# An expert's last 96 slots as moving columns, fills on another engine, a bound taken by matmul, and a new written order

## The chip, the cores and the metric

The kernel runs on one core of one Trainium2 chip. A core has a matmul engine (TensorE, PE in the rows; its weight loads are listed apart as PEld), a vector engine (VectorE, DVE), an activation engine (ScalarE, ACT), a general engine (GpSimd, POOL) and a queue engine (SyncE, SP) that issues most of the transfers. Each engine works through its own list of instructions in order and waits on semaphores for the others. The metric is the device time of one execution in microseconds (us); the kernel before took 974.89 us as the median of three runs (974.52 to 978.32).

## The reference

Three stages follow one another.

```python
# 1. attention: B=4, H=8, S=576, D=64, pooled by 4 and local in a band
out_d = sm_attn(q_d, k_d, v_d)                 # q, k, v averaged over 4 positions
out_up = np.repeat(out_d, 4, axis=2)
mask = np.abs(pos[:, None] - pos[None, :]) < 4
out_local = softmax(where(mask, q @ k.T / 8, -1e9)) @ v
x = (out_up + out_local) laid out as 2304 tokens x 512
# 2. a dense layer, 512 -> 2048 -> 512
x = maximum(x @ w_in, 0) ** 2 @ w_out
# 3. eight experts, 512 -> 1024 -> 512, the two best of a noisy gate per token
noisy = x @ w_gate + log1p(exp(x @ w_noise)) * noise
for e in range(8):
    out[mask] += top2_w[mask] * (maximum(x[mask] @ w1[e], 0) @ w2[e])
```

The inputs q, k, v and the dense weights are 64 bits wide where they are doubles; the attention inputs are read as 32 bits, the dense weights are turned from 64 to 32 bits on the chip.

## The kernel before

All matmuls of the layers are done with operands that are split into two 16-bit parts, a high and a low one, so that each product takes three matmuls (high by high, high by low, low by high). The scale of each operand comes from a bound on its size. For the two weights of the dense layer and for v this bound is a sum of squares or the largest element of a Gram matrix.

*First stage and dense layer.* One program text, the string `ORDER`, sets in which order the pieces are issued; every engine then has its instructions in that order. A piece is a letter code and a number. `qk`, `vg`, `vw` load inputs; `G` averages q and k; `S` and `D` are the score matmuls of a unit (batch, pair of heads, half of the sequence); `ml`, `md`, `el`, `ed`, `nl`, `nd` are its softmax; `PT` transposes the probabilities, `PW` multiplies them with v, `xb` writes the two halves of x. `vm` takes the bound of v, `vs` its sums, `Xa`, `Xm`, `Xb` make its scale. `il`, `ia`, `ib`, `ic`, `ij` turn one eighth of w_in from 64 to 32 bits (load, two VectorE and two ScalarE steps), `in` adds its Gram matrix, `is` takes the maximum, `wS`, `wT`, `wU` make the scale s_in, `wh` and `wl` write the high and the low half of one eighth of the columns. `ol` to `oo` do the same for w_out. `M` i is the first matmul of the dense layer for one of 72 steps (9 chunks of 256 tokens, 8 groups of 256 hidden columns each), `r` its ReLU and square, `yh` and `yl` the second matmul of chunk 0 in pieces by columns, `Y` and `Z` that of the other chunks. `ga` to `gg` are the gate of one of 18 tiles of 128 tokens: scale, split, transpose (by TensorE and a ScalarE copy for the last tile, L728 and L729), logits (`gd`, L740), a polynomial for log1p(exp) (`gf`), the two best, their slots (`ge`, the prefix sums at L800 and L802) and the scatter of the row into a table in device memory that has 608 slots for each expert.

*Experts.* Expert 0 starts inside `ORDER`: `pe` pieces split its weights, `cm` are its first layer (8 column groups for the first 384 slots, 8 for the last 224) and `cw` its second layer on single tiles of 128 slots, while the last gate tiles still run. Experts 1 to 7 are a plain loop behind it, whose instructions are put in order by the framework's scheduler. For each expert the first layer (L932) runs over 16 pieces, ScalarE and VectorE write the halves of h from PSUM (L934, L935), and between them the weights of the next expert are squared (L861, which waits for their transfer) and split (L877, L878). Then `c_m2` is called for j = 0 to 4, four tiles of 128 slots and one of 96:

```python
for f in range(8):
    do = slice(f * DM, f * DM + DM)
    for a, bb in ((hh, wh), (hh, wl), (hl, wh)):
        nc.tensor.matmul(po, a[:, f, jo], bb[:, do], start=(i == 0), stop=(i == 23))
```

The slots are the stationary operand there and 512 weight columns move, whatever the number of slots. VectorE scales the result with the slot's weight (L950), GpSimd scatters it with an adding transfer (L951). The last tile of expert 7 is done in two halves of 256 columns (`last_m2`, L975 to L979). A final branch for experts with more than 608 slots is not taken.

*Start.* `constants()` makes index ramps, masks and the identity on VectorE and then fills five tiles that must be zero outside what is written later (L159 to L162).

Of the kernel before, what the change touches and what calls it, by code (L numbers as in the profile page):

```python
# [24 lines left out]
E = 8  # L25
# [32 lines left out]
oB2 PW3 in7 oa3 is7 el5 oc2 wS0 ml6 wT0 ol1 oj2 wU0 xb3 oa0 wh1 oB0 oB3 vw5 nl5 wh5 wl1 oc0 oj0 wh0 wl0 os0 wh3
oc3 oj3 oa1 qk4 oB1 os2 wl5 wh2 wl3 wh6 wh7 os3 el6 M5 oc1 oj1 qk5 wl7 ed6 of3 ra5 os1 wh4 nl6 M0 wl6 wl4 vm5
wl2 S7 r0 of1 PW4 nd5 oh2 oo2 ol5 oh3 oh0 vs5 oo3 M1 ra1 ol6 oh1 oo0 G4 D7 M4 ol7 PT5 xb4 nd6 yh0 yl9 M3 r4 md7  # L60
ra3 PW5 yl1 yl0 yh9 oa5 M6 oa6 oo1 yl13 oB5 ml7 ol4 xb5 r6 yl8 yl11 yl3 oa7 S8 yl12 PT6 yl4 ed7 el7 oB6 vg6 M2
oB7 yh6 yh8 ml8 oc5 nl7 yh4 M7 oj5 yh13 oc6 D8 oc7 oj6 yh11 oj7 yh3 oa4 vm6 yh1 oB4 os7 os5 yh14 vw6 md8 yl14
nd7 oc4 os6 qk6 yl6 oj4 S9 of7 PW6 ed8 os4 yh5 oh7 yl5 yh12 qk7 G5 oh6 of5 yh30 vw7 oo7 yh28 vw8 S11 yh27 oh5
oh4 vs6 yh24 yh25 oo5 yh22 PT7 D9 oo4 yh19 oo6 yh20 yh16 xb6 PW7 r2 yh29 yh17 SD0 xb7 yl22 yl29 yl16 yl28 yl24
ml9 vg7 el8 md9 pz0 nl8 yl25 vm7 yh21 yl30 M13 yh2 Xa1 nd8 el9 yl17 G7 ra7 M9 yl18 ed9 D11 yl27 nl9 yh10 Xm1 S10
G6 Xb1 yl2 yh31 nd9 yh15 ra13 pg0 md11 yh18 yh7 vs7 yl10 PT8 D10 PT9 vw9 ip0 ml11 pf0 ra9 md10 ml10 M12 ip1 r12
el10 nl10 yl15 ed10 PW8 yl7 el11 M11 pf1 M10 nd10 ed11 pf2 pf3 yh23 ra11 S12 xb8 D12 yl21 md12 vg8 yl26 nl11 r10
PT10 PW9 ml12 pf4 yl20 M15 vm8 S13 nd11 xb9 el12 vw10 PT11 ml13 D13 ed12 PW10 pf5 md13 vw11 nl12 ra15 M14 xb10
PW11 S15 M8 ed13 el13 S14 nl13 yl23 nd12 r14 pf6 nd13 xb11 r8 D15 PT12 yh26 M16 vw12 yl31 ml14 pf7 zo0 vs8 ra16
el14 md15 PT13 yl19 ga0 gb0 D14 M17 PW12 M19 nl14 ga1 Y8 md14 gc0 Y9 Y10 ml15 Y11 vw13 gb1 ed14 el15 gd0 Y12 vg9  # L70
qk8 nd14 ed15 vw14 Y13 Y14 qk9 vm9 gf0 G8 xb12 G9 ge0 ra17 S16 gc1 gd1 gg0 nl15 M23 vs9 S17 PW13 nd15 Y15 ra19
ra23 qk10 xb13 PT14 vw15 M22 PT15 D16 vg10 ga2 M18 gf1 gb2 ge1 gg1 ra22 PW14 ml16 gc2 qk11 ra18 vm10 ga3 D17
# [27 lines left out]
def moe_kernel(ctx, tc, qk_in, vwin, vgrp, w_in, w_out, w_gate, w_noise, noise, w1, w2, out):  # L100
# [95 lines left out]
    def load_vg(b, hp):  # L196
        if hp == 0:
            vd[b] = ap.tile([72, NP, 4, 64], F32, tag="vd", name=f"vd{b}")
            vmx[b] = ap.tile([P, H], F32, tag="vmx", name=f"vmx{b}")
            nc.vector.memset(vmx[b], 1.0e-30)  # L200
# [840 lines left out]
    def win_pieces():  # L1041
# [343 lines left out]
```

## Time and profile before

| | |
|---|---|
| median of three runs | 974.89 us |
| the profiled execution | 974.24 us, of which the span of its instructions is 972.5 us |
| TensorE busy | 916.3 us (94%) |
| VectorE busy | 580.7 us (60%) |
| ScalarE busy | 498.9 us (51%) |
| GpSimd busy | 132.4 us (14%) |
| transferred | 121.17 MB, mean 125 GB/s |

The span runs from the first to the last instruction; the execution's own time is 1.74 us longer. A share of busy time is an average: the table says that TensorE is nearly always at work, and not where it isn't. The rows further down are stretches, single instructions and pieces of the chain of work that ended last. In them a time in front is the start in us from the span's start, the next is the length of the row, and a bracket gives the idle time of that engine before the row and what ended it. Matmuls are pipelined and the end of each is modelled, so what a matmul costs the next one is read from the distance of starts.

### The profile page before, as it was taken

The numbers are of one execution on the slowest core, as the hardware profiler recorded it, in microseconds if no ns is written. First come the engines' busy times: TensorE is split into PE (matmuls) and PEld (weight loads), VectorE is DVE, ScalarE is ACT, GpSimd is POOL, SyncE is SP. The second block draws the span as 40 slices with busy tenths as digits, with TensorE's granted clock in tenths as the row PEclk, the third lists the DMA queues.
The fourth block names the chain that finished last, engine by engine and source line by source line (L and its number), as shares of the span: only waits on it lengthen the run. The fifth ranks groups of instructions, "written<-read, shape, count | busy, mean of one in ns | idle before, by whom it ended". The sixth has DMA issues, their size and how long they took to land.

```text
span 972.5 us, 20336 instructions
## 1 busy us (share of the span) xinstructions
PE 916.3 (94%) x8278; PEld 619.0 (64%) x8278; DVE 580.7 (60%) x1812; ACT 498.9 (51%) x1076; POOL 132.4 (14%) x151
## 2 busy tenths in 40 slices
PE   4549999999999899999999979999999999999997
PEld 2437988675766567676757546746565565656574
DVE  7989887488678666566477765543435262626221
ACT  5688767455466455455744472753626263624010
POOL 2501100011102010010111121020111111110203
PEclk9768999999999999999999999999999999999999
DMA  9942587923241502013411748771847667590304
GB/s 290 337 147 97 169 262 287 240 90 86 88 101 58 86 30 49 21 61 96 161 56 36 226 122 222 122 206 20 221 56 204 73 187 90 158 119 10 43 1 55
DMA packets 103143, 121.17 MB, mean 125 GB/s; under 512 B 68256, under 2 KB 68448, under 8 KB 100992
## 3 DMA queue, kind: packets, MB, share of 16 engines
q1 hardware_dynamic: 94544, 100.30, 38.0%
q0 software_dynamic: 8496, 19.48, 10.0%
q8 instruction: 67, 1.10, 0.5%
q14 instruction: 36, 0.29, 0.1%
HBM read 70.33 MB, written 35.02 MB: 108 GB/s over the span
## 4 chain that ended last, share of the span: by engine, by line
PE 65%; DVE 4%; ACT 2%; DMA 1%; issue 0%; POOL 0%; POOLq 0%; ACTq 0%; DVEq 0%
PE po L948 20%; PE phc L932 19%; PE y L663 11%; PE ph L617 11%; DMA xs<-row,si 1%; ACT xall L861 1%; PE px L429 1%; PE px L421 1%; PE pol L975 1%; PE S L310 0%; PE S L295 0%; PE pfr L479 0%; PE ptp L375 0%; PE pl L740 0%; ACT r L636 0%
## 5 line engine op out<-in xcount | busy, mean ns | idle before, releaser
L617 PE MATMUL ph<-xall,wih 128*128 128x256 f16 x1152 | 196.1, 276 | 0.6 <-ACT r L636 0.4
L932 PEld LDWEIGHTS <-we 128*128 128x128 f16 x1536 | 148.5, 98 | 50.7
L948 PE MATMUL po<-we,h 128*128 128x512 f16 (+1 forms) x816 | 177.3, 379 | 0.0
L617 PE MATMUL ph<-xall,wil 128*128 128x256 f16 x576 | 158.6, 275 | 2.0 <-DVE wil L1095 2.0
L932 PE MATMUL phc<-xT,we 128*128 128x384 f16 (+1 forms) x1152 | 150.6, 293 | 0.0
L948 PEld LDWEIGHTS <-h 128*128 128x128 f16 (+1 forms) x816 | 83.4, 102 | 91.2
L663 PE MATMUL y<-wo,gh 128*128 128x512 f16 x448 | 133.3, 379 | 0.0
L617 PEld LDWEIGHTS <-wih 128*128 128x128 f16 x1152 | 111.1, 99 | 18.4 <-issue 1.9
L934 ACT ACTIVATE h<-phc 128x384 f16<-128x384 f32 (+1 forms) x112 | 47.3, 423 | 135.3 <-PE phc L932 135.3
L950 DVE TENSOR_SCALAR ob<-po,om 128x512 f32<-128x512 f32 (+1 forms) x34 | 25.5, 749 | 122.8 <-PE po L948 122.8
L832 POOL DMA_INDIRECT xs<-row,si x36 | 38.6, 1072 | 403.1 <-issue 110.3
L951 POOL DMA_INDIRECT out_dram<-ob,tk x34 | 52.3, 1538 | 298.6 <-DVE ob L950 284.2
L935 DVE SCALAR_TENSOR_TENSOR h<-phc,h 128x384 f16<-128x384 f32 (+1 forms) x112 | 52.2, 470 | 64.9 <-ACT h L934 64.9
L663 PE MATMUL y<-wo,gl 128*128 128x512 f16 x224 | 84.9, 379 | 0.3 <-DVE gl L646 0.3
L663 PEld LDWEIGHTS <-gh 128*128 128x128 f16 x448 | 42.1, 98 | 44.6 <-issue 1.0
L646 DVE TENSOR_TENSOR gl<-g,gh 128x512 f16<-128x512 f32 x64 | 44.3, 693 | 39.7 <-ACT gh L645 39.3
L617 PEld LDWEIGHTS <-wil 128*128 128x128 f16 x576 | 56.9, 99 | 9.8 <-DVE wil L1095 2.5
L636 ACT ACTIVATE r<-ph 128x512 f32<-128x512 f32 x72 | 42.2, 586 | 13.2 <-PE ph L617 13.0
L640 ACT ACTIVATE g<-r 128x512 f32<-128x512 f32 x72 | 45.4, 630 | 2.3
L861 ACT ACTIVATE junk<-w1raw 128x1024 bf16<-128x1024 f32 x24 | 25.4, 1056 | 36.4 <-DMA w1raw<-in_moe_w_dram 25.8
L878 DVE SCALAR_TENSOR_TENSOR we<-w1raw,sce,we 128x1024 f16<-128x1024 f32 x32 | 40.6, 1278 | 2.7 <-ACT we L877 2.7
L878 DVE SCALAR_TENSOR_TENSOR we<-w2raw,sce,we 128x1024 f16<-128x1024 f32 x32 | 40.6, 1275 | 0.9 <-ACT we L877 0.9
(354 smaller groups left out, 1382.3 us busy)
## 6 DMA issues: line engine op xcount, KB each, us to landing
w1raw<-in_moe_w_dram SPq DMA_DIRECT2D x8, 2048.0 KB
w2raw<-in_moe_w_dram SPq DMA_DIRECT2D x8, 2048.0 KB
xs<-zrow SPq DMA_DIRECT2D x8, 1290.0 KB
qkT<-in_qk_dram SPq DMA_DIRECT2D x16, 579.0 KB
raw<-in_moe_w_out_dram SPq DMA_DIRECT2D x8, 1024.0 KB
out_dram<-zrow SPq DMA_DIRECT2D x1, 4864.0 KB
raw<-in_moe_w_in_dram SPq DMA_DIRECT2D x4, 1024.0 KB
vw<-in_vwin_dram SPq DMA_DIRECT2D x48, 76.0 KB
```

The costliest lines, as they stand in the source:

```text
L617: nc.tensor.matmul(ph[:, f], a[:, kk, fo], bb[:, kk], start=(n == 0), stop=(n == 11))
L636: nc.scalar.activation(r, ph, AF.Relu, scale=KAPPA)
L640: nc.scalar.activation(g, r, AF.Square)
L646: nc.vector.tensor_tensor(gl, g, gh, op=OP.subtract)
L663: nc.tensor.matmul(py[c, tt], a[:, o], bb[:, ft], start=(ft == 0 and n == 0), stop=(ft == 15 and n == 2))
L832: st = nc.gpsimd.indirect_dma_start(out=xs, out_offset=bass.IndirectOffsetOnAxis(ap=si[:, kk:kk + 1], axis=0), in_=roww, in_offset=None)
L878: nc.vector.scalar_tensor_tensor(wl[:, o], raws[i][:, o], ss[i], wh[:, o], op0=OP.mult, op1=OP.subtract)
L932: nc.tensor.matmul(ph[:, :n], a[:, fo], xT[:, bb], start=(i == 0), stop=(i == 11))
L934: nc.scalar.activation(hh[:, f], ph[:, :n], AF.Relu)
L935: nc.vector.scalar_tensor_tensor(hl[:, f], ph[:, :n], 0.0, hh[:, f], op0=OP.max, op1=OP.subtract)
L948: nc.tensor.matmul(po, a[:, f, jo], bb[:, do], start=(i == 0), stop=(i == 23))
L951: st = nc.gpsimd.indirect_dma_start(out=out, out_offset=bass.IndirectOffsetOnAxis(ap=tk[:m], axis=0), in_=ob[:m], in_offset=None, compute_ ...
```

## The change

Five things are changed.

- The second layer of the tile of 96 slots of experts 1 to 7 is done the other way round. `part_m2` takes 128 weight columns as stationary operand and moves the 96 slots, in four groups of 24 matmuls, into one PSUM bank (`poT`). ScalarE copies the result (`yt`), `part_rows` transposes it back with four matmuls against the identity (`poR`), and VectorE and GpSimd go on as before. The tiles are taken in the order 0, the matmuls of the 96 slots, 1, their transposes, 2, 3; expert 7 ends with tile 3 in two halves.
- The five fills of `constants()` run on GpSimd.
- The bound of v for batch 0 is the largest element of a Gram matrix of the 72 rows, made by 32 matmuls into one PSUM tile, in place of eight squares on ScalarE.
- The Gram matrices of w_in go into one PSUM tile instead of four, so one maximum is taken in place of four and one over them; the bound of a quarter of w_out is a maximum and no longer a sum over the diagonal.
- `ORDER` is written anew, with the gate's `gf` split into `gx`, `gy` and `gz`.

```diff
@@ ORDER, first line and the lines about the last gate tile
-vg0 vg3 ob0 qk0 vg2 S0 vg1 vm0 qk1 qk2 vm1 vm2 G0 S1 ml0 G1 D0 md0 ml1 el0 vg4 ed0 S2 vm3 G2 vm4 el1 D1 il0 Xa0
+qk0 vg0 G0 qk1 S0 S1 ml0 D0 G1 il0 el0 nl0 vg2 qk2 D1 ml1 md0 ed0 vm0 nd0 vg4 md1 ia0 vg1 el1 S2 ed1 ib0 S4 G2
...
-gc17 le1 cm1 gd17 ge16 gx17 cm6 pe17 gg16 gy17 gz17 cm5 pe18 ge17 gg17 cm4 pe19 pe20 cm3 pe21 pe22 pe23 pe24 cw1
+cm2 gx16 cm7 gc17 gy16 cm0 gz16 le1 cm1 gd17 gx17 cm6 ge16 gy17 cm5 gg16 gz17 cm4 cm3 ge17 gg17 pe17 pe18 pe19
@@ constants()
         nc.gpsimd.memset(pms[0], 0.0)
+        for i in range(2):
+            nc.gpsimd.memset(pTs[i][0], 0.0)
+            nc.gpsimd.memset(vws[i][32:64], 0.0)
...
-        nc.vector.memset(pms[1], 0.0)
-        for i in range(2):
-            nc.vector.memset(pTs[i][0], 0.0)
-            nc.vector.memset(vws[i][32:64], 0.0)
+        nc.gpsimd.memset(pms[1], 0.0)
@@ vg_max, x_scale
+        v = vg.rearrange("g a b -> g (a b)").bitcast(BF16).rearrange("g (f n w) -> g f n w", n=P, w=2)[:, :, :, 1]
+        for f in range(8):
+            nc.tensor.matmul(pv0[:, :P], v[:, f], v[:, f], start=(seen_v[0] == 0), stop=(seen_v[0] == 31))
+            seen_v[0] += 1
...
-        nc.vector.tensor_reduce(m1, vmx[b], AX.X, OP.max)
+        nc.vector.tensor_reduce(m1, vmx[b] if b else pv0[:, :P], AX.X, OP.max)
@@ second layer of the 96 slots
+    def part_m2(e, hh, hl):
+        _, (wh, wl) = WE[e][0]
+        jo = slice(NR * P - P, CAP)
+        m = CAP - jo.start
+        po = ps2.tile([P, DM], F32, tag="m2", name="poT")
+        for d in range(4):
+            i = 0
+            for f in range(8):
+                do = slice(f * DM + d * P, f * DM + d * P + P)
+                for a, bb in ((wh, hh), (wh, hl), (wl, hh)):
+                    nc.tensor.matmul(po[:, m * d:m * d + m], a[:, do], bb[:, f, jo], start=(i == 0), stop=(i == 23))
+                    i += 1
+        yt = cp.tile([P, 4, m], F32, tag="yt", name="yt", bufs=1)
+        nc.scalar.activation(yt.rearrange("p d m -> p (d m)"), po[:, :4 * m], AF.Copy)
+        return yt
+
+    def part_rows(e, yt, om, tk, ob):
+        m = CAP - (NR * P - P)
+        pt = psT.tile([P, 512], F32, tag="tp", name="poR")
+        for d in range(4):
+            nc.tensor.transpose(pt[:m, P * d:P * d + P], yt[:, d], idf)
+        nc.vector.tensor_scalar(ob[:m], pt[:m], om[:m], None, op0=OP.mult)
+        scatter(e, tk, ob, m)
@@ Gram matrices of w_in and w_out
-                nc.tensor.matmul(pn[i][:, P * (f % 4):P * (f % 4) + P], v[:, f], v[:, f], start=i in fresh,
-                                 stop=done_[i] == 16)
+                nc.tensor.matmul(pn[:, P * (f % 4):P * (f % 4) + P], v[:, f], v[:, f], start=done_[0] == 1,
+                                 stop=done_[0] == 64)
...
-            for i in (2 * c, 2 * c + 1):
-                nc.vector.tensor_reduce(top[:, i:i + 1], pn[i], AX.X, OP.max)
+            if c:
+                nc.vector.tensor_reduce(top, pn, AX.X, OP.max)
...
-                nc.vector.scalar_tensor_tensor(pq[:, P:2 * P], pq[:, :P], 1.0, idf, op0=OP.mult, op1=OP.mult,
-                                               accum_out=acc[q_][:, c:c + 1])
+                nc.vector.tensor_reduce(acc[q_][:, c:c + 1], pq[:, :P], AX.X, OP.max)
@@ loop over experts 1 to 7
-        for j in range(NR):
+        for j in (0, NR - 1, 1, NR, 2, 3):
+            if j == NR - 1:
+                yt = part_m2(e, hh, hl)
+                continue
             ob = cp.tile([P, DM], F32, tag="ob", name="ob", bufs=3)
-            if e == E - 1 and j == NR - 1:
+            if j == NR:
+                j = NR - 1
+                part_rows(e, yt, om[:, 1, j:j + 1], tk[:, j:j + 1], ob)
+            elif e == E - 1 and j == 3:
                 last_m2(e, j, hh, hl, om[:, 1, j:j + 1], tk[:, j:j + 1], ob)
-                continue
-            c_m2(e, j, hh, hl, om[:, 1, j:j + 1], tk[:, j:j + 1], ob)
+            else:
+                c_m2(e, j, hh, hl, om[:, 1, j:j + 1], tk[:, j:j + 1], ob)
```

VectorE at the start, before: `pm`, `pT` and `vw` are the five filled tiles, `qkT` is the first q and k.

```order
L158 TENSOR_SCALAR idf<-pm_91,pidx 128x128
L159 MEMSET pm_91 128x320
L161 MEMSET pT_92 128x512
L162 MEMSET vw_96 32x768
L161 MEMSET pT_94 128x512
L162 MEMSET vw_97 32x768
L163 CAST onesb<-onesf 128x128
L268 TENSOR_REDUCE qkT_0_186<-qkT_0_186 128x288
```

And now:

```order
L163 TENSOR_SCALAR idf<-pm_91,pidx 128x128
L165 CAST onesb<-onesf 128x128
L281 TENSOR_REDUCE qkT_0_178<-qkT_0_178 128x288
L336 TENSOR_REDUCE mx<-S 128x4
L337 TENSOR_TENSOR pm_90<-S,mx 128x4x38
```

The five fills are gone from this list and stand on GpSimd's; the first q and k is also the first transfer that SP issues, where two groups of v stood ahead of it.

ScalarE at the last two gate tiles, before: `yT` is the transposed row of the last tile, `e` the exponential of a tile's two best (the first of tile 16, the second of tile 17), `wih` the first layer of expert 0, `ex` an exponential inside the gate.

```order
L747 ACTIVATE ex<-na 128x8
L934 ACTIVATE wih<-phc 128x384 x2
L790 ACTIVATE e_8463<-dd 128x1
L934 ACTIVATE wih<-phc 128x384
L729 COPY yT<-pty 128x1024
L934 ACTIVATE wih<-phc 128x384
L747 ACTIVATE ex<-na 128x8
L934 ACTIVATE wih<-phc 128x384
L861 ACTIVATE xall,acce_8568<-w1raw_8491 128x1024
L790 ACTIVATE e_8606<-dd 128x1
```

And now:

```order
L760 ACTIVATE ex<-na 128x8
L947 ACTIVATE wih<-phc 128x384 x2
L742 COPY yT<-pty 128x1024
L947 ACTIVATE wih<-phc 128x384
L803 ACTIVATE e_8496<-dd 128x1
L947 ACTIVATE wih<-phc 128x384
L760 ACTIVATE ex<-na 128x8
L947 ACTIVATE wih<-phc 128x384 x2
L803 ACTIVATE e_8624<-dd 128x1
L947 ACTIVATE wih<-phc 128x384 x2
```

The copy `yT` stands ahead of the exponential of tile 16. On TensorE the transposes of the last tile stand behind two groups of expert 0's first layer instead of three, two groups instead of one lie between them and the logits of that tile, and four groups instead of two between those logits and its prefix sums.

ScalarE at an expert's second layer, now: `we` is the split of the next expert's weights, `junk` the squares of the one after it, which read `w1raw` and `w2raw` from a transfer, `h` the first layer.

```order
L890 ACTIVATE we_9220<-w2raw_8935,sce_9195 128x1024
L874 ACTIVATE junk,acce_9556<-w1raw_9327 128x1024 x3
L989 ACTIVATE yt<-poT 128x384
L874 ACTIVATE junk,acce_9556<-w1raw_9327 128x1024
L874 ACTIVATE junk,acce_9557<-w2raw_9329 128x1024 x4
L947 ACTIVATE h_9016<-phc 128x384 x8
```

The new copy stands behind three squares; before, the eight squares stood there with nothing between them. Experts 6 and 7 have no squares ahead of it.

## Rows read from the trace of the kernel before

**Rows 1.** The page: busy time, share of the span and instructions of each engine.
```profile
PE 916.3 (94%) x8278; PEld 619.0 (64%) x8278; DVE 580.7 (60%) x1812; ACT 498.9 (51%) x1076; POOL 132.4 (14%) x151
```

**Rows 2.** Busy time by stretch: PE, PEld, DVE, ACT, POOL, clock, transfer share, GB/s.
```profile
0.00:80.00 80.00, 40.50 (x540) 29.57 (x541) 68.27 (x136) 56.08 (x106) 20.80 (x27) 0.77 0.71 238
80.00:550.00 470.00, 465.88 (x5163) 336.06 (x5162) 334.28 (x1263) 269.41 (x667) 44.49 (x76) 1.00 0.39 111
550.00:570.00 20.00, 14.66 (x117) 8.93 (x114) 14.97 (x84) 7.63 (x18) 2.16 (x4) 1.00 0.57 217
570.00:972.50 402.50, 395.26 (x2469) 244.44 (x2467) 163.15 (x331) 165.82 (x286) 64.99 (x44) 1.00 0.55 113
```

**Rows 3.** Chain that ended last, in the expert loop: start, length, what.
```profile
633.73 25.90 PE po L948 x120
...
786.96 25.90 PE po L948 x120
```

**Rows 4.** Timeline of TensorE at full clock: matmuls of 128, 128 (f32) and 16 columns.
```profile
91.61 0.38 PE L375 MATMUL ptp<-idf,pm 128*102 128x128 f32 x2
91.83 0.27 PE L377 MATMUL ptp<-idf,pm 128*38 128x128 f32 x1
...
100.46 1.06 PE L687 MATMUL y<-wo,gh 128*128 128x128 f16 x16
101.35 0.23 PE L288 MATMUL S<-masks,idb 128*128 128x152 bf16 x1
...
549.79 0.45 PE L740 MATMUL pl<-wgs,yT 128*128 128x16 f16 x12
550.10 6.01 PE L932 MATMUL phc<-wih,we 128*128 128x384 f16 x36
```

**Rows 5.** Timelines of ScalarE and VectorE around an expert's second layer.
```profile
637.66 0.38 DVE L935 SCALAR_TENSOR_TENSOR h<-phc,h 128x224 f16<-128x224 f32 x1
...
667.47 0.49 ACT L934 ACTIVATE h<-phc 128x384 f16<-128x384 f32 x1 [1.46 <-PE phc L932]
...
798.14 1.06 ACT L861 ACTIVATE junk<-w1raw 128x1024 bf16<-128x1024 f32 x1
```

**Rows 6.** Timelines of TensorE, ScalarE, SP at the last two gate tiles.
```profile
560.96 0.46 PE L740 MATMUL pl<-wgs,yT 128*128 128x16 f16 x12 [2.45 <-ACT yT L729]
568.27 0.17 PE L800 MATMUL pr<-ohs,trib 128*128 128x8 bf16 x1 [2.88 <-DVE ohs L786]
588.78 9.36 PE L932 MATMUL phc<-xall,we 128*128 128x224 f16 x96
...
559.42 0.20 ACT L790 ACTIVATE e<-dd 128x1 f32<-128x1 f32 x1 [4.66 <-DVE dd L788]
559.90 1.00 ACT L729 COPY yT<-pty 128x1024 f16<-128x1024 f16 x1
...
575.96 1.52 SPq L900 DMA_TRANSPOSE xall<-xs  x1
```

**Rows 7.** Timelines of the start: VectorE, then TensorE.
```profile
5.68 0.33 DVE L159 MEMSET pm<- 128x320 f32 x1
8.29 0.70 DVE L162 MEMSET vw<- 32x768 f32 x1 [0.19 <-issue]
9.16 1.34 DVE L268 TENSOR_REDUCE qkT<-qkT 128x288 f32<-128x1152 f32 x1
54.92 1.28 DVE L1071 TENSOR_REDUCE top<-pn 128x1 f32<-128x512 f32 x2
63.79 0.15 DVE L174 TENSOR_SCALAR s_in<-es 128x1 int32<-128x1 int32 x1
...
8.31 0.73 PE L295 MATMUL S<-qkT 64*32 64x38 f32 x32 [2.59 <-DMA qkT<-in_qk_dram]
75.44 0.40 PE L617 MATMUL ph<-xall,wil 128*128 128x256 f16 x1 [2.00 <-DVE wil L1095]
79.82 1.10 PE L1120 MATMUL pq<-raw 128*128 128x128 bf16 x8
```

More of the change, by code (lines that the diff above doesn't have):

```diff
@@ L58 @@
[L58 to L72, printed above, removed]
@@ new lines @@
+PW25 PT26 nd27 ml28 ra41 D29 M44 md28 el28 md29 xb25 M47 gb9 vw27 PT27 vw26 ed29 gb8 ml29 ed28 nl28 PW26 vw28
+gc8 Y40 ra44 el29 xb26 Y41 Y42 PW27 S30 xb27 Y43 nd28 D30 ra47 nl29 gd8 Y44 PT28 md30 gx8 gy8 gz8 vw29 nd29 Y45
+gc9 gd9 M48 gx9 gy9 gz9 ge8 S31 gg8 M49 ra49 Y46 ed30 ge9 PW28 Y47 D31 ml30 ra48 ga10 PT29 gg9 el30 md31 M51
+gb10 M50 nl30 xb28 gc10 ml31 nd30 ra51 ra50 ga11 PW29 el31 M53 gb11 M55 xb29 gd10 Y48 ra53 PT30 M52 ed31 nl31
+Y49 gc11 nd31 ra55 Y50 ra52 vw30 gd11 vw31 Y51 gx10 gy10 gz10 PT31 Y52 gx11 gy11 gz11 PW30 xb30 M54 PW31 ge10
@@ L198, in load_vg @@
             vd[b] = ap.tile([72, NP, 4, 64], F32, tag="vd", name=f"vd{b}")
+        if hp == 0 and b:
             vmx[b] = ap.tile([P, H], F32, tag="vmx", name=f"vmx{b}")
@@ L209, in moe_kernel @@
     vgs = {}
+    pv0 = ps1.tile([P, 512], F32, tag="m1", name="pv0")
+    seen_v = [0]
     def vg_max(b, hp):
         vg = vgs[b, hp]
-        for i in range(2):
-            jv = sp.tile([P, 512], BF16, tag="jv", name="jv", bufs=1)
-            nc.scalar.activation(jv[:72], vg[:, 2 * i:2 * i + 2].rearrange("g a b -> g (a b)"), AF.Square,
-                                 accum_out=vmx[b][:72, 2 * hp + i:2 * hp + i + 1])
+        if b:
+            for i in range(2):
+                jv = sp.tile([P, 512], BF16, tag="jv", name="jv", bufs=1)
+                nc.scalar.activation(jv[:72], vg[:, 2 * i:2 * i + 2].rearrange("g a b -> g (a b)"), AF.Square,
+                                     accum_out=vmx[b][:72, 2 * hp + i:2 * hp + i + 1])
+            return
+        v = vg.rearrange("g a b -> g (a b)").bitcast(BF16).rearrange("g (f n w) -> g f n w", n=P, w=2)[:, :, :, 1]
+        for f in range(8):
+            nc.tensor.matmul(pv0[:, :P], v[:, f], v[:, f], start=(seen_v[0] == 0), stop=(seen_v[0] == 31))
+            seen_v[0] += 1
     def vg_sum(b, hp):
-        vg = vgs.pop((b, hp))
+        vg = vgs[b, hp]
         eng = nc.vector if b else nc.gpsimd
@@ L1042, in win_pieces @@
         vi = wx.tile([P, 4, FF], F32, tag="wo", name="vi")
-        pn = [ps1.tile([P, 512], F32, tag="m1", name=f"pn{i}") for i in range(2)]
-        pn += [ps2.tile([P, 512], F32, tag="m2", name=f"pm{i}") for i in range(2)]
-        top = sp.tile([P, 4], F32, name="top", bufs=1)
-        fresh = set(range(4))
-        done_ = [0] * 4
+        pn = ps1.tile([P, 512], F32, tag="m1", name="pn")
+        top = sp.tile([P, 1], F32, name="top", bufs=1)
+        done_ = [0]
         wih = wp.tile([P, 4, FF], F16, tag="wih", name="wih")
```

74 lines of the change are left out of this document (42 added, 32 removed).

## The prediction

> **What bounds the kernel now.** I read the page first. TensorE is busy for 916.3 us of the span, the next engine for 580.7 [rows 1]. So the reader is to look for two things only: where TensorE is not at work, and what its work costs. The busy times by stretch answer the first. Of 972.5 us TensorE is idle for about 39.5 in the first 80, 4.1 in the next 470, 5.3 between 550 and 570, and 7.2 in the rest, most of it behind the last matmul [rows 2]. VectorE is busy for 68.3 of the first 80 us and the clock there is 0.77 on the mean [rows 2]: the start is bound by VectorE and ScalarE, which prepare the weights. Between 80 and 550 us and in the expert loop TensorE sets the pace at full clock, so work taken from another engine there is worth nothing. The chain of waits shows the expert loop as matmuls in one piece: 120 of a second layer in 25.90 us, 0.2158 us each for 512 columns [rows 3]. So three places can move the end: the start, the last gate tiles, and the matmul work of seven second layers.
>
> **Seven second layers.** Removed are 24 matmuls of 512 columns, 24 x 0.2158 = 5.18 us [rows 3]. (Expert 7's halved tile costs the same for 128 slots as for 96, since the columns count.) Added are 96 matmuls of 96 columns, each with a weight load of its own, and four transposes. No row has 96 columns with such a load. Above stands the one with 128 columns and a load for each: 16 of them from 100.46 to 101.35, 55.6 ns each; below the one with 16 columns and a full load: 12 from 549.79 to 550.10, 26 ns each [rows 4]. From 128 to 512 columns a column costs (215.8 - 55.6)/384 = 0.417 ns. If 55.6 were set by the load, 96 columns would cost the same; but a load with almost no columns is done in 26 ns, so the columns set it, and I take 55.6 - 32 x 0.417 = 42.3 ns, nearest the upper row. 96 x 42.3 = 4.06 us. Two transposes of 128 columns in f32 take 91.83 - 91.61 = 0.22 us [rows 4], four 0.44. The sum is 4.50 against 5.18: 0.68 us less for each expert, 4.8 for seven. With 55.6 ns it would be 0.60 more for each, 4.2 in all; with 26 ns 2.24 less, 15.7 in all.
>
> Sixteen pairs of load and matmul at 128 columns ran here at 55.6 ns each, one behind the other [rows 4]. The Trainium skill speaks against that: its page "TensorE: Matmul & The Clock Gate", section "Back-to-back issue gap", gives about 81 ns for a pair at 128 columns in a stream, because the load counts, and about 56 ns only for an isolated matmul. The trace does not agree with the 81. By the page's 81 ns the 96 would take 7.8 us and the change would cost 3.0 us for each expert; by the rows it gains 0.68.
>
> What the new pieces wait for. The matmuls of the 96 slots read the halves of h that VectorE writes last: its last one ends at 638.04, the second layer starts at 633.73, and the new matmuls start one tile later, at 638.9 [rows 3, 5]: no wait, with 0.9 us in hand. The copy `yt` on ScalarE is queued behind three squares that wait for the transfer of `w1raw`; in the latest expert the third of them ends at 799.2, 12.2 us into a second layer that began at 786.96 [rows 3, 5]. A copy of this shape takes 0.49 us [rows 5], so it is done at 12.7. Needed it is when tile 1 ends, 5.18 + 4.06 + 5.18 = 14.4 us in: there the transposes want it, and tile 2 wants the PSUM bank. What is queued behind it on ScalarE is five squares that nobody waits for. So the copy costs nothing as long as `w1raw` lands no more than 1.7 us later than in that expert; each us beyond is a us of TensorE.
>
> **The last two gate tiles.** TensorE waits 2.45 us for the copy `yT` and 2.88 us for the prefix sum's input of tile 17 [rows 6]. The copy waited in ScalarE's queue behind the exponential of tile 16, which started at 559.42 [rows 6]; in the new order it is ahead of it and two groups of expert 0's first layer, 1.95 us each by 36 matmuls from 550.10 to 555.94, cover it [rows 4, 6]. That wait goes. What is late next is VectorE: it still has all of tile 16 to do before tile 17's logits, so the input of the last prefix sum comes at about 568 as before. But four groups now lie ahead of it instead of two, so TensorE gets there with 3.9 us more done. I take 4.2 us for both waits; 5.3 is the most that is there, and none would be won if the late rows of expert 0 came later than TensorE: they are asked for at 575.96 and used at 588.78 [rows 6]; 4.2 us earlier leaves them 8.6.
>
> **The start.** Three things leave VectorE ahead of the scale s_in, which is done at 63.94 [rows 7]. The five fills with their gaps, 5.68 to 8.99, and the average of the first q and k starts at 9.16, right behind; that q and k had landed by 8.31 as the third transfer [rows 7] and is the first now, so VectorE can go on some 3 us earlier, and GpSimd has nothing else to do then. Of the maxima four of 0.64 us become one, 1.9 us; and the smaller one over them. Not all of it arrives at s_in: the same bytes of w_in have to land, and transfers take 0.71 of the first 80 us [rows 2]. Between 0 and 6 us I take 4. The first dense step followed s_in by 75.44 - 63.94 = 11.5 us, and eight long VectorE instructions lie between in the old list and seven in the new; I leave the 11.5, so M0 starts at about 71.4 instead. By then TensorE has in its list about as much behind it as before at 79.82, when the first step was done [rows 7]: that step is gone from it, but the score, transpose and value matmuls of four units have moved ahead. That is 8.4 us; a first step at the low clock costs some 2.2 more than at the high one (its last 21 matmuls took 4.4 us [rows 7]; by 0.42 ns a column 24 take 2.6), and I leave 1.2 for the second half of w_out, whose loads now stand behind two more of q and k on SP's queue. That gives 5.0 us, between 0 and 8. The 32 matmuls for the bound of v lie in the 39.5 idle us of TensorE; if that cover failed they would hold the scores up by some 3 us. The eight squares that leave ScalarE are off the path early in the start, and the maxima of w_out are VectorE work of the same cover: nothing for either.
>
> **The middle.** From 80 to 550 us the same matmuls come in another order. Only 4.1 us of idle time is there to win [rows 2]; new waits could cost more. The loads of the engines up to each dense step differ little between the two lists, so I take 0, between -3 and +8.
>
> **The sum.** 974.24 - 4.8 - 4.2 - 5.0 = 960.2 us against the profiled execution; the median of the runs is 0.65 above that execution, so the forecast is 960.8 us.
>
> **The rivals.**
> - *The start gives nothing*: s_in is held by w_in's landing or by ScalarE, or TensorE waits later for what was not ready sooner. For it: the busy transfers; against it: VectorE is the one that is nearly full. 974.9 - 4.8 - 4.2 = 965.9.
> - *More than I count*: the start gives 8 us, the idle time of the middle goes too. 974.9 - 4.8 - 5.3 - 8 - 3 = 953.8.
> - *The middle takes it back*: in the new order a score or a dense step meets a full VectorE queue again and again. The old order has 4.1 us of this in 470 [rows 2], and a planned order is unlikely to have four times as much; 8 to 14 us of waits would give 969 to 975.
> - *Slower: the weight loads show.* In `part_m2` a load comes every 96 columns. If a pair takes more than (5.18 - 0.44)/96 = 49.4 ns the part loses, and beyond about 70 ns it eats the other 9.2 us and the kernel is slower by over 0.5%. At 81 ns: 974.9 - 9.2 + 7 x 3.0 = 986.7. Against it stand the 55.6 and the 26 ns [rows 4], both with the same kind of load.
> - *The change does not do what it says*: `yt` comes late each time because `w1raw` lands later. With 3 us more than the latest expert showed, five experts lose 1.3 each, 6.5 in all: 967.3.
>
> **How the numbers follow.** Forecast 0.56, with a range of its own of 955 to 966; nothing at the start 0.14; more than counted 0.12; middle 0.08; `yt` late 0.04; loads show 0.06. What a measurement can tell from no change is about 0.5%, 4.9 us. Below 970.0 lie the forecast, the start, more than counted, `yt` late and some of the middle's: 0.89, of which I take 0.05 off for what I have not seen: 0.84. Within 0.5%: 0.09. Slower: 0.07. The range that holds 8 in 10 goes from the far side of "more" to the middle of the middle's: 951 to 971.
>
> **What would show it.** Right: an expert's period shorter by 0.6 to 0.8 us, starts of `poT` matmuls 42 ns apart, no wait ahead of `poR`; no wait for `yT` and under 1 us ahead of the last prefix sum; s_in done near 60 and M0 near 71. Wrong: `poT` starts over 50 ns apart, an idle TensorE ahead of `poR` put down to `yt`, s_in later than 63, or over 8 us of idle TensorE between 80 and 550.

## The result, and the profile after

The changed kernel takes 985.29 us (median of 5 runs, 982.26 to 986.38); the kernel before, on the same chip, 978.32 (974.52 to 979.88). The ratio is 1.0068, interval 1.0048 to 1.0089: slower, with the interval's lower end just under the 0.5% that the prediction took as what can be told. Forecast were 960.8 us, and faster. A second timing, e0_after_again, beside its own runs of the kernel before, gave 1.0064 (1.0046 to 1.0082).

The page and the stretches of the kernel after, answering to [rows 1] and [rows 2]. Columns of a stretch: PE, PEld, DVE, ACT, POOL, clock, transfer share, GB/s.

```profile
PE 924.8 (94%) x8842; PEld 639.8 (65%) x8842; DVE 577.8 (59%) x1794; ACT 496.0 (50%) x1067; POOL 132.6 (13%) x156
```

```profile
0.00:80.00 80.00, 48.56 (x674) 36.86 (x675) 66.79 (x130) 52.93 (x96) 23.36 (x34) 0.75 0.74 253
80.00:550.00 470.00, 455.25 (x4988) 330.95 (x4987) 323.70 (x1236) 259.52 (x651) 40.85 (x74) 0.99 0.36 106
550.00:570.00 20.00, 20.00 (x119) 10.24 (x118) 14.52 (x34) 11.04 (x17) 0.00 (x0) 1.00 0.63 179
570.00:983.60 413.60, 400.95 (x3067) 261.76 (x3065) 172.78 (x397) 172.53 (x304) 68.36 (x48) 0.99 0.52 115
```

The idle time of TensorE between 80 and 550 us went from 4.1 to 14.8, that behind 570 from 7.2 to 12.7. It fell from 39.5 to 31.4 in the first 80 us, where TensorE has 134 more matmuls to do, and from 5.3 to 0 between 550 and 570. So the span is 11.1 us longer with only 2.6 more of idle time: most of the rest is work at a lower clock, and a table of idle time alone does not show the loss. The expert loop came as forecast. The chain of work that ended last, answering to [rows 3]:

```profile
640.83 8.07 PE phc L945 x84
648.90 5.18 PE po L961 x24
654.08 4.08 PE poT L986 x96
658.16 5.18 PE po L961 x24
663.34 0.44 PE poR L996 x4
663.78 10.36 PE po L961 x48
674.14 16.75 PE phc L945 x108
```

Pieces follow each other without a gap: 96 pairs of a weight load and a matmul in 4.08 us (42.5 ns each), the four transposes in 0.44, no wait ahead of them. What is lost lies ahead of expert 1: its first layer starts at 623.56, before at 608.40. The waits of TensorE from 80 to 625 us say where. A row names the engine and line that waited, what ended the wait, the us in total, how many times and the longest:

```profile
PE px L442 <- DMA vw<-in_vwin_dram: 9.1, 3, 4.9
PE phc L945 <- DVE xall L948: 4.2, 1, 4.2
PE pr L813 <- DVE ohs L799: 1.8, 2, 1.1
```

In the kernel before, no `px` waited for such a transfer behind 80 us (its 6.2 us lie in the start), and no `phc` for VectorE. The stretches with the three long waits:

```profile
120.00:130.00 10.00, 5.68 (x95) 4.99 (x89) 8.18 (x15) 7.25 (x14) 2.12 (x8) 0.95 0.32 70
130.00:140.00 10.00, 9.39 (x119) 9.05 (x120) 5.06 (x13) 2.79 (x8) 0.00 (x0) 0.71 0.74 243
340.00:350.00 10.00, 7.12 (x77) 4.53 (x75) 3.56 (x12) 3.79 (x12) 0.00 (x0) 0.88 0.14 53
350.00:360.00 10.00, 10.00 (x103) 5.13 (x101) 7.46 (x32) 3.12 (x11) 0.00 (x0) 0.95 0.23 57
600.00:610.00 10.00, 5.80 (x46) 5.07 (x44) 9.22 (x12) 6.61 (x11) 2.61 (x1) 0.85 0.74 161
```

These waits cost more than themselves, because the granted clock falls behind them: 0.71 on the mean from 130 to 140 us, so part of that work ran at 1.2 in place of 2.4 GHz, an estimated 0.29 x 9.39 = 2.7 us.

**First wait.** Value loads (`vw`) share two buffers, even numbers one and odd numbers the other, and SP issues transfers in the order of its list. The old list had vw7 ahead of vw8, the new one has vw8 first. Timeline of SP (three windows), then of TensorE; rows of SP last as long as issuing:

```profile
108.38 0.59 SPq L271 DMA_DIRECT2D vw<-in_vwin_dram  x2
...
120.30 0.23 SPq L271 DMA_DIRECT2D vw<-in_vwin_dram  x1
120.92 0.61 SPq L271 DMA_DIRECT2D vw<-in_vwin_dram  x2
```

```profile
125.18 0.50 PE L434 MATMUL px<-pTd,vd 72*64 72x80 f32 x8
130.61 1.12 PE L442 MATMUL px<-pT,vw 102*64 102x64 f32 x16 [4.92 <-DMA vw<-in_vwin_dram]
```

At 108.38 vw6 is issued. vw8 has to wait until PW6 has read vw6, at 120.3. vw7, whose buffer PW5 had left at 99.5, stands behind it, is asked for at 120.92 and has not landed when PW7 wants it.

**Second wait.** vw22 stands behind the transposing transfer of gate tile 6, which SP issues at 336.46, when its row is ready. TensorE is ready for PW22 at 343.0, 4.6 us behind the issue of vw22 at 338.39, and waits:

```profile
336.46 1.24 SPq L744 DMA_TRANSPOSE yT<-row  x1
337.79 0.50 SPq L209 DMA_DIRECT2D vg<-in_vgrp_dram  x1
338.39 1.50 SPq L271 DMA_DIRECT2D vw<-in_vwin_dram  x4
```

```profile
345.89 0.69 PE L442 MATMUL px<-pT,vw 102*64 102x64 f32 x16 [2.88 <-DMA vw<-in_vwin_dram]
```

**Third wait.** VectorE's timeline at the late rows of expert 0 (`lr1`; `mt` is their small table, `we` the split weights of expert 1, `xall` here a half of expert 0's h), and TensorE's:

```profile
592.59 0.75 DVE L963 TENSOR_SCALAR wil<-po,om 128x512 f32<-128x512 f32 x1 [4.43 <-PE po L961]
597.39 0.23 DVE L929 SCALAR_TENSOR_TENSOR om<-mt 128x2 f32<-128x2 f32 x2 [4.05 <-DMA mt<-xs]
...
599.81 2.48 DVE L891 SCALAR_TENSOR_TENSOR we<-w1raw,sce,we 128x1024 f16<-128x1024 f32 x2 [0.39 <-ACT we L890]
602.87 2.47 DVE L891 SCALAR_TENSOR_TENSOR we<-w1raw,sce,we 128x1024 f16<-128x1024 f32 x2
605.25 1.28 DVE L891 SCALAR_TENSOR_TENSOR we<-w2raw,sce,we 128x1024 f16<-128x1024 f32 x1
606.45 0.68 DVE L948 SCALAR_TENSOR_TENSOR xall<-phc,xall 128x224 f16<-128x224 f32 x2
```

```profile
606.89 6.42 PE L945 MATMUL phc<-xall,we 128*128 128x224 f16 x48 [4.20 <-DVE xall L948]
```

The rows themselves had landed: TensorE used them from 597.93 on. It is VectorE that stands still for the table with five weight splits behind it, and the drain of TensorE's sums behind those. This wait differs between executions: in the trace of e0_after_again, the same kernel, it is shorter, and no low clock follows it (1.00 from 600 to 620 us), while the waits for `vw` loads come to 8.2 us there too:

```profile
PE phc L945 <- DVE xall L948: 2.6, 1, 2.6
```

**The start.** s_in came at 63.99, before at 63.79 [rows 7]. The first dense step began at 77.03, before at 72.84, with more score and value work ahead of it (before, then after):

```profile
72.84 0.61 PE L617 MATMUL ph<-xall,wih 128*128 128x256 f16 x2
77.03 0.60 PE L630 MATMUL ph<-xall,wih 128*128 128x256 f16 x2
```

### The profile page after: what moved, and what is told of

Read it like the earlier page. It is cut to its first block, busy times and chain, and to the rows that moved or that the text cites. A ratio compares the mean times of both kernels' runs of the same rounds, so it can differ in the third digit from the quotient of the medians.

```text
span 983.6 us, 21447 instructions
## 1 busy us (share of the span) xinstructions
PE 924.8 (94%) x8842; PEld 639.8 (65%) x8842; DVE 577.8 (59%) x1794; ACT 496.0 (50%) x1067; POOL 132.6 (13%) x156
## 3 DMA queue, kind: packets, MB, share of 16 engines
q0 software_dynamic: 8528, 19.48, 9.8%
## 4 chain that ended last, share of the span: by engine, by line
PE 44%; DVE 3%; DMA 1%; ACT 1%; issue 1%; POOL 0%; SPq 0%; POOLq 0%; ACTq 0%
PE phc L945 18%; PE po L961 15%; PE y L676 3%; PE ph L630 3%; PE poT L986 3%; DMA xs<-row,si 1%; DVE we L891 1%; DMA mt<-xs 0%; ACT xall L874 0%; PE poR L996 0%; DVE wil L948 0%; POOL out_dram L1020 0%; PE pol L1016 0%; SPq L913 0%; PE pfr L492 0%
## 5 line engine op out<-in xcount | busy, mean ns | idle before, releaser
L630 PE MATMUL ph<-xall,wih 128*128 128x256 f16 x1152 | 193.9, 274 | 1.6 <-ACT r L649 1.6
L961 PE MATMUL po<-we,h 128*128 128x512 f16 x648 | 143.3, 379 | 0.0
L961 PEld LDWEIGHTS <-h 128*128 128x128 f16 x648 | 63.0, 98 | 71.6
L845 POOL DMA_INDIRECT xs<-row,si x36 | 36.6, 1017 | 418.5 <-ACT r L649 148.8
L963 DVE TENSOR_SCALAR ob<-po,om 128x512 f32<-128x512 f32 x27 | 20.2, 750 | 118.8 <-PE po L961 118.8
```

The source lines that it names most:

```text
L630: nc.tensor.matmul(ph[:, f], a[:, kk, fo], bb[:, kk], start=(n == 0), stop=(n == 11))
L845: st = nc.gpsimd.indirect_dma_start(out=xs, out_offset=bass.IndirectOffsetOnAxis(ap=si[:, kk:kk + 1], axis=0), in_=roww, in_offset=None)
```

## The experiments

Theory: the new second layer and the new gate tail gain what was forecast, and three misplaced tokens of the list cost more. Rivals: the new arrangement of the middle is slow as a whole (a mended token only moves the hole); or the parts of the start cost time. All runs, each set against the kernel before on its own chip:

| run | what | us | ratio to before (95%) | s_in | expert 1 starts |
|---|---|---|---|---|---|
| changed kernel | | 985.29 | 1.0068 (1.0048-1.0089) | 63.99 | 623.56 |
| e0_after_again | the same | 984.25 | 1.0064 (1.0046-1.0082) | 65.02 | 620.63 |
| e1_layer2_only | before + second layer | 971.38 | 0.9964 (0.9949-0.9978) | 64.14 | 608.74 |
| e2_vw7 | changed, vw7 ahead of vw8 | 977.41 | 1.0023 (1.0010-1.0036) | 63.57 | 620.17 |
| e3_lr1 | changed, lr1 later | 980.67 | 1.0057 (1.0035-1.0079) | 64.02 | 617.28 |
| e4_vw22 | changed, vw22 earlier | 980.02 | 1.0023 (1.0006-1.0040) | 64.53 | 617.97 |
| e5_three | all three | 966.93 | 0.9919 (0.9900-0.9938) | 63.98 | 603.62 |
| e5_again | the same | 967.10 | 0.9884 (0.9866-0.9902) | 65.11 | 610.31 |
| e7_fills_late | e5, fills later | 967.18 | 0.9900 (0.9878-0.9921) | 65.07 | 605.91 |
| e8_pieces_first | e5, pieces ahead of PW1 | 968.18 | 0.9899 (0.9881-0.9916) | 63.82 | 604.30 |
| e9_both | e7 and e8 | 967.97 | 0.9902 (0.9885-0.9919) | 64.42 | 603.89 |
| e10_vw1 | e9, vw1 earlier | 970.41 | 0.9921 (0.9904-0.9937) | 67.71 | 608.84 |
| e11_tail | e1 + new tail | 968.65 | 0.9908 (0.9892-0.9924) | 62.17 | 605.18 |
| e12_v_scalar | e5, bound of v on ScalarE | 967.34 | 0.9893 (0.9876-0.9910) | 66.06 | 606.35 |
| e13_fills_vector | e5, fills on VectorE | 967.17 | 0.9895 (0.9877-0.9912) | 65.12 | 604.14 |
| e14_two_mb | e5, 2 MB more in the queue | 971.88 | 0.9948 (0.9930-0.9966) | 68.09 | 609.69 |

The last two columns, both in us from the span's start, come from the one profiled execution of a run, and executions differ: e5 reached expert 1 at 603.62 and, a second time, at 610.31. So verdicts go by the ratios, and the trace only says which wait is there.

**e1_layer2_only.** The kernel before with `part_m2`, `part_rows`, `scatter` and the new loop over tiles.

> The kernel before with nothing but the new second layer (tiles in the order 0, the 96 slots, 1, their transposes, 2, 3); list of tokens and start as before. Theory: the second layer does in the old list what it does in the new one, 0.66 us for each of seven experts (period 50.41 against 51.07), so 4.6 us less than the kernel before, a ratio near 0.995. Rival: in the old list the copy of the 96 slots' sums comes too late for the transposes, and TensorE waits ahead of poR; then within 1.5 us of the kernel before.

Measured: 0.36% faster (0.22 to 0.51), 3.5 us. Within the interval of the 4.6; the second layer does its part in either list.

**e2_vw7, e4_vw22, e3_lr1.** One token each:

```diff
-PW6 of5 oh6 vw8 oo7 yh28 yl14 D9 vs6 oh5 vw7 yh30
+PW6 of5 oh6 vw7 oo7 yh28 yl14 D9 vs6 oh5 vw8 yh30
-vw21 nd22 ... gb6 gc6 xb21 Y32 PT22 S24 ml24 vg15 vw22 G14
+vw21 vw22 nd22 ... gb6 gc6 xb21 Y32 PT22 S24 ml24 vg15 G14
-cw0 lr1 pe25 pe26 pe27 cw2
+cw0 pe25 pe26 pe27 lr1 cw2
```

> The changed kernel with two tokens exchanged: the load vw7 ahead of vw8, as in the list before. Theory: vw8 waits on SP's queue for a buffer that PW6 frees at 120.3, and vw7, whose buffer is free from 99.5, stands behind it; asked at about 109 it is there for PW7 at 125.5. The wait of 4.9 us goes and with it most of the stretch at half clock behind it (about 3 us): 7 to 8 us less than the changed kernel, 977 to 978. Rival: the load is slow because of what else moves then (weights, noise), and PW7 or PW8 waits as long as now: less than 2 us.

> The changed kernel with one token moved: vw22 right behind vw21, so ahead of the transposing transfer of gate tile 6 on SP's queue. Theory: the load, whose buffer PW20 frees near 311, is asked near 313 in place of 338.4 and is there for PW22 at 342.5; the wait of 2.9 us goes and with it the low clock behind it (1 to 1.5 us): about 4 us less than the changed kernel, ratio to the kernel before near 1.002. Rival: the gate tile's transfer or the copy of a dense step takes its place: less than 1.5 us.

> The changed kernel with one token moved: lr1 (late rows of expert 0) behind pe25 to pe27. Theory: VectorE idles 4.05 us for the late rows' small table with five weight splits of expert 1 behind it in the queue, and the drains of phc stand behind those; with scales and two splits ahead of that wait the drains come 4 us earlier: the 4.2 us wait of TensorE goes and the low clock behind it (about 2 us), 4 to 6.5 us less than the changed kernel, 979 to 981. Rival: the transposed rows themselves land too late, and TensorE then waits for their transfer in place of VectorE: less than 1.5 us.

The waits went in all three. Timeline of TensorE and a stretch of e2, where vw7 is now asked at 108.77:

```profile
124.88 0.50 PE L434 MATMUL px<-pTd,vd 72*64 72x80 f32 x8
125.20 0.64 PE L442 MATMUL px<-pT,vw 102*64 102x64 f32 x16
```

```profile
130.00:140.00 10.00, 10.00 (x134) 8.81 (x132) 8.63 (x24) 7.24 (x19) 0.00 (x0) 1.00 1.03 375
```

Neither a wait nor a fallen clock is left there. By the ratios e2 gains 0.45% (4.4 us) against the changed kernel, not 7 to 8; that its median lies in the 977 to 978 of the expectation is luck, since the kernel before took 974.55 us beside it and 978.32 beside the changed one. Part is taken back by a dense step that waits longer for ScalarE (1.2 us at most in the changed kernel), and by the clock behind it (waits of e2 from 80 to 600 us, then a stretch):

```profile
PE ph L630 <- ACT r L649: 3.4, 3, 2.9
```

```profile
480.00:490.00 10.00, 7.07 (x45) 5.26 (x44) 2.14 (x3) 7.83 (x15) 0.00 (x0) 0.69 0.14 29
```

This profiled execution, 982.05 us, is the slowest of e2's twelve, so what the others lose there is not shown.

e4 gains 0.45% as expected (4 us); PW22 runs at 342.02 without a wait. e3's trace has no wait at the late rows any more (from 600 to 610 us TensorE is busy for 9.87, in the changed kernel 5.80), yet its ratio is only 0.11% better, inside the uncertainty of the two (0.3%): by time it is unclear what lr1 alone is worth.

**e5_three.** All three.

> The changed kernel with three tokens in other places: vw7 ahead of vw8, vw22 right behind vw21 (in place of behind the transposing transfer of gate tile 6), lr1 behind pe27. Theory: the waits are independent and their gains add: 7.5 + 5 + 2.9 and about 1 of low clock = 16 us less than the changed kernel, about 969. Rival: what an earlier stretch gains the next wait takes back (gate copies, later value loads): 975 or more.

Measured: 0.9919 and 0.9884, so 0.8 to 1.2% faster than the kernel before and 1.5 to 1.8% (14 to 18 us) faster than the changed one. The gains add up, to even more than the single runs let expect (0.45 + 0.45 + 0.1%). The traces fit that in kind: e2, with one token moved, still lost clock from 330 to 350 us (0.86 and 0.80) behind the wait for vw22 and from 480 to 490, and e5 shows a clock of 1.00 from 80 to 550. How much of it is that is open. Of idle time 6.8 us are left in the middle, against 4.1 in the kernel before. Stretches of e5:

```profile
80.00:550.00 470.00, 463.20 (x5058) 333.44 (x5056) 334.03 (x1251) 267.18 (x660) 41.29 (x74) 1.00 0.38 109
550.00:570.00 20.00, 18.88 (x141) 11.32 (x138) 15.62 (x87) 7.61 (x19) 1.99 (x3) 1.00 0.54 204
570.00:963.60 393.60, 386.23 (x2977) 253.17 (x2975) 161.27 (x329) 168.48 (x293) 65.32 (x46) 1.00 0.52 116
```

**e11_tail.** The second layer and the new list's last 84 tokens (with lr1 moved) in the old list.

> The kernel before with the new second layer and with the last 84 tokens of the list (from dense step 67 on: last output tiles, gate tiles 16 and 17, expert 0) in the order of the kernel with three tokens moved; start and middle as before. Theory: the gate tail gives in the old list what it gives in the new one, 4.2 to 4.6 us, beside 3.5 to 4.6 for the second layer: 8 to 9 us less than the kernel before, ratio 0.991 to 0.992, no wait for yT and under 1.5 us ahead of the last prefix sum. Rival: the tail only pays with the steps that the new list puts ahead of it; then 0.995 to 0.997, as with the second layer alone.

Measured: 0.9908, so 0.56% (5.5 us) better than e1. Waits of e11 from 540 to 620 us, all of them:

```profile
PE pr L800 <- DVE ohs L786: 1.1, 1, 1.1
```

The 2.45 us for `yT` are gone and 1.1 of 2.88 are left [rows 6]: 4.2 us, as forecast. And the old start and middle do as well as the new ones: 0.9908 here, 0.9884 to 0.9919 for e5.

**The start: e7, e8, e9, e10, e12, e13.** All on e5.

```diff
@@ e7: constants()                       (e9: with e8's order; e13: the five fills on VectorE as before)
-        for i in range(2): nc.gpsimd.memset(pTs[i][0], 0.0); nc.gpsimd.memset(vws[i][32:64], 0.0)
...
         nc.gpsimd.affine_select(trib, onesb, ...)
+        for i in range(2): nc.gpsimd.memset(vws[i][32:64], 0.0); nc.gpsimd.memset(pTs[i][0], 0.0)
@@ e8: ORDER
-ed3 PW1 ia2 il3 il4 ic1 S5 ... il6 ib2 ij1 D5
+ed3 ic1 ia2 ij1 ib2 PW1 il3 il4 S5 ... il6 D5
@@ e10: ORDER of e9
-vw0 vs0 ... nl3 vw1 ml4
+vw0 vw1 vs0 ... nl3 ml4
@@ e12: vg_max and x_scale as in the kernel before
```

> The kernel with three tokens moved (966.9), with GpSimd's four fills behind its affine_select, so from about 6 us on in place of 1.25 to 3.94. Theory: while GpSimd fills, VectorE's small adds that build the row of indices take 0.65 to 0.76 us in place of 0.17, each ending as a fill ends; with the fills later the first identity is done near 5.1 in place of 7.1 us, and up to 2 us of it reach the scale s_in (64.1) and the end: 0 to 2 us less. Rival: the fills then stretch what VectorE does from 6 us on just as much: idb early, but the first q and k averages late, and nothing at s_in.

> The kernel with three tokens moved, with four steps on pieces 1 and 2 of w_in (ic1, ia2, ij1, ib2) ahead of PW1 in place of behind it. Theory: the queues of ScalarE and VectorE stand still for 2.5 and 2.4 us near 32 to 34 us behind PW1's two reads of its sums, which wait for the transfer of vw1; the steps that now lie ahead fill this, VectorE (nearly full from 35 to 64) gets to s_in 2 to 2.5 us earlier, at about 62, and the end comes 1.5 to 2.5 us earlier. Rival: piece 2 has not landed by then either, or the scores that PW1's step now holds up on VectorE are what TensorE needs: no gain, or up to 2 us more.

> Both edits of the start together, on the kernel with three tokens moved. Theory: the gains add, s_in near 60.5 to 62 and the end 2 to 4 us earlier (963 to 965), which is what the prediction had counted for the start. Rival: w_in's transfers bind the start, s_in stays at 63 to 64 and the end within 1.5 us.

> The kernel with three tokens moved and both edits of the start, and vw1 right behind vw0, so ahead of the second to eighth megabyte of w_in on SP's queue (now asked at 15.2 behind two of them and landed at 33.2). Theory: PW1 waits 3.2 us for it on TensorE, at the low clock, and scores that VectorE waits for 3.5 us stand behind it; with the load early these waits go, s_in comes at 61 to 62 in place of 64.4, the first dense step at 74 to 75 in place of 77.5, and the end 2 to 3 us before the kernel with three tokens moved. Rival: w_in's own transfers or the serial steps on its eight pieces bind s_in, as in the two runs before: s_in at 63.5 or later, end within 1.5 us.

> The kernel with three tokens moved, with the bound of v by ScalarE's squares again (eight of 0.8 us) in place of TensorE's 32 matmuls (4.2 us of TensorE at the start). Theory: both lie beside the transfers that set s_in, so nothing changes: within 2 us of the kernel with three tokens moved, ratio 0.987 to 0.992. Rival one: the matmuls cost TensorE up to 4.2 us; then 2 to 4 us faster. Rival two: the squares hold up w_in's pieces on ScalarE; then 2 to 4 us slower, s_in at 66 or later.

> The kernel with three tokens moved, with the five fills on VectorE again. Theory: what VectorE does ahead of 35 us does not reach s_in, which w_in's transfers and the serial steps on its eight pieces set: s_in at 64 to 66, within 2 us of the kernel with three tokens moved. Rival: the fills cost what the prediction had counted, 3 us of VectorE ahead of s_in: s_in at 66.5 to 68 and 2 to 3 us slower.

The theories of e7, e8, e9 and e10 fell. In e7 the adds are quick again and the identity is begun at 5.07 in place of 6.90, yet s_in came at 65.07; e8 moved four steps into the gap of the two queues, and s_in stayed at 63.82. e9 shows where the time went, in VectorE's waits from 0 to 64 us:

```profile
DVE mx L335 <- PE S L322: 4.1, 2, 3.5
DVE qkT L280 <- DMA qkT<-in_qk_dram: 2.3, 1, 2.3
```

VectorE, spared work, waits longer. In e10 the wait of PW1 for vw1, 3.2 us, went and another transfer came late in its place (TensorE's waits from 0 to 82 us), and s_in moved out to 67.71:

```profile
PE S L307 <- DMA qkT<-in_qk_dram: 6.1, 3, 3.4
```

That execution of e10 also had TensorE at full clock over all of its first 80 us, where the changed kernel's mean was 0.75, so the low clock is not what holds s_in back:

```profile
0.00:80.00 80.00, 48.06 (x627) 36.06 (x627) 61.15 (x126) 49.32 (x91) 21.33 (x34) 1.00 0.73 252
```

e12 takes the 32 matmuls (4.19 us) out of the first 80 us, e13 puts 3 us on VectorE, and neither changes the time: the cover that the prediction named for the 32 matmuls and the squares was there.

**e14_two_mb.** Two transfers of 1 MB that nobody reads, ahead of the second piece of w_in.

```diff
+    more = dpool.tile([2, P, 2048], I32, name="more_dram")
+        "du": lambda n: nc.sync.dma_start(more[n], w_out[n].bitcast(I32)),
-... il1 el3 il2
+... du0 du1 il1 el3 il2
```

> The kernel with three tokens moved, with two more transfers of 1 MB each (a copy of w_out's first two pieces that nobody reads) ahead of the second piece of w_in on SP's queue. Theory: transfers bind the start (share 0.99 between 20 and 40 us, 368 GB/s), so 2 MB more push s_in out by 5.5 us or more (by 368 GB/s; up to 11 if a copy takes the engines twice), to 69.5 to 76, and the end by about as much. Rival: the serial steps on w_in's pieces bind, and the transfers have slack: s_in at 64 to 66, end within 2 us.

Measured: s_in at 68.09, 3.0 and 4.1 us later than in the two profiles of e5, and 0.47% slower than their mean (4.6 us). The load vw1 shows it best, for which PW1 waited 3.2 us in the changed kernel:

```profile
37.28 1.12 PE L442 MATMUL px<-pT,vw 102*64 102x64 f32 x16 [7.46 <-DMA vw<-in_vwin_dram]
```

s_in moved by less than the 5.5 us that 2 MB take at 368 GB/s (e5's second profile, 20 to 40 us), so a little slack is there; the rest goes into s_in and into the end.

## Why the prediction was wrong

Two of its own signs of being wrong are in the trace: s_in later than 63 (63.99) and over 8 us of idle TensorE between 80 and 550 (14.8).

- **Second layer: right.** 42.5 ns for a pair (42.3 taken), 4.08 + 0.44 us in place of 5.18 (4.50 forecast), a period of 50.41 (from 674.14 to the next first layer at 724.55) against 51.07; no wait for `yt`. The Trainium skill, "TensorE: Matmul & The Clock Gate", section "Back-to-back issue gap", gives N/2.4 + 2.5 ns for an isolated matmul, 42.5 at 96 columns, and expects a stream of pairs to be slower: here a stream of 96 runs at just that gap. The rival "the weight loads show" (986.7) came near the measured time by chance; its mechanism is not there.
- **Gate tiles: right for the two waits** (4.2 us; e11 gives 5.5 with its uncertainty of about 2), **wrong behind them.** The step "4.2 us earlier leaves them 8.6" looked at the late rows' transposes alone. The new list also put their table's wait on VectorE ahead of five weight splits; that took 4.2 us back in one trace of the changed kernel and 2.6 in the other, and by time e3 leaves its worth unclear. An instruction that waits is not alone on its engine: what stands behind it had to be read from the order, and was not.
- **Start: the step of 5.0 us failed.** It took VectorE, busy for 68.3 of 80 us, as the bound, and weighed "the same bytes of w_in have to land" only as a discount, by the mean transfer share of 0.71. By stretches the start has two halves: from 20 to 40 us the transfers were full (share 0.99 in the kernel before, first row), from 40 to 60 VectorE is (19.48 of 20 us in the changed kernel, second row):

```profile
20.00:40.00 20.00, 14.07 (x254) 10.13 (x256) 16.68 (x36) 13.67 (x31) 9.45 (x11) 0.83 0.99 367
40.00:60.00 20.00, 8.48 (x76) 6.88 (x77) 19.48 (x25) 16.02 (x29) 8.02 (x6) 0.59 0.75 262
```

  Three edits that spare VectorE or fill its gaps (e7, e8, e9) and one that loads it (e13) moved s_in by hardly more than executions differ, and 2 MB more of transfers moved it by 3 to 4 us. All four act on what VectorE does ahead of about 40 us, so that work does not set s_in, and the transfers have little slack. Whether VectorE or the transfers hold the half behind 40 us was not tested: no run spared VectorE there. Two terms of the step were off besides. "Some 3 us earlier" was 1.5 (the first average starts at 7.62 in place of 9.16), because the fills slowed VectorE from GpSimd, as shown at the end. And the 11.5 us from s_in to the first dense step were counted from 75.44, where that step went on after a wait; it had begun at 72.84, and in the changed kernel it began 12.9 us behind s_in. The rival "the start gives nothing" was right for this part: its 965.9 is 0.9908 of 974.9, and e5, with the three tokens mended, measured 0.9884 to 0.9919.
- **Middle: the step "I take 0, between -3 and +8" failed, and the largest part of the loss is here.** It compared the engines' loads up to each dense step and not the list of SP, where vw7 had changed places with vw8 and vw22 had come to stand behind a gate tile's transfer. In the trace these are 4.9 and 2.9 us of waits with 2.7 and, at 0.88 and 0.95 of the clock, about 1.4 us of low clock behind them: 11.9. The rival "the middle takes it back" had the right size (8 to 14 us) and a small chance (0.08), but another mechanism: it had a full VectorE queue in mind, and what came late were loads on SP's list.

Added up from the trace: 960.2 + 5.0 (start) + 11.9 (two loads) + 4.2 and 0.9 of low clock (late rows, 0.15 x 5.80) = 982.2 us. The 960.2 were set against the profiled execution, and that took 985.29 us, so some 3.1 us stay without a place; the low clock terms are estimates. By time, the three tokens are 14 to 18 us (e5), which leaves about the start's 5.0 to the forecast.

## What to carry to other kernels

Where a list of work is written anew, compare the queue that issues the transfers line by line: on an in-order queue, a load whose buffer is free is as late as the one ahead of it whose buffer is not, and loads that share buffers want to stand in the order in which they are used. The wait for one transfer costs what stands behind it on that engine and, on TensorE, often a stretch at half clock as well: here 4.9 us of wait brought 2.7 more. An engine that is 85% busy over a stage need not be the bound of all of it: look at the shares in shorter stretches, spare it where it is full, and load the other suspect, as the 2 MB did in one run. Three tokens mended give a kernel that is 0.8 to 1.2% faster than the one before.

## What the runs showed of the hardware

Fills on GpSimd slowed VectorE. In the changed kernel five adds of 1 to 16 columns took 3.00 us together, the last four each ending within 0.03 us of one of GpSimd's fills; in the kernel before, with those fills not on GpSimd, 0.98. VectorE's row first, then GpSimd's:

```profile
0.97 3.00 DVE L147 TENSOR_SCALAR pm<-pm 128x1 f32<-128x1 f32 x5
...
1.84 0.73 POOL L141 MEMSET vw<- 32x768 f32 x1
2.63 0.52 POOL L140 MEMSET pT<- 128x512 f32 x1
```

In e7 the same fills ran from 6.35 to 9.04 beside VectorE's averages and maxima, which took 1.34 and 0.31 us as without them, and the five adds took 0.98. The Trainium skill, "SBUF — State Buffer", section "Who interferes with whom", says that the two engines share one pair of ports as an exclusive lock, which VectorE's `tensor_scalar` can take in its modes with two ports and its reductions never do; both halves agree with these rows, which do not show the mode of the adds. By e13, where the fills are on VectorE and the time is the same, it cost nothing that could be told at the end.
